# Transposes ahead of the old y products in a group's turn, logits inside it, half of x's row moves from Scalar, and a respacing of the side work

## The chip, the cores and the metric

The kernel runs on one core of a Trainium2 chip. The metric is the device time of one launch in microseconds (us), the median of several runs. TensorE (PE) multiplies matrices, VectorE (DVE), ScalarE (ACT) and GpSimd (POOL) do elementwise work, and SyncE (SP) issues DMAs. All five run their own instruction streams in order, and wait for one another on semaphores.

## The reference, cut to what matters

```
# 1. RWKV-like scan: B=4, H=8, S=768 steps, head width D=48
for t in range(S):
    cur = u * k_t outer v_t
    y[t] = r_t @ (state + cur)
    state = w_t[:, None] * state + k_t outer v_t
x = y.transpose(0, 2, 1, 3).reshape(3072, 384)
# 2. first MoE block: a gated product
x = ((x @ w1) * (x @ w2)) @ w3 @ w_out
# 3. second MoE: logits x @ w_gate -> P by 8 rounds of row and column scaling
for e in range(8):
    out += P[:, e:e+1] * (relu(x @ w1[e]) @ w2[e])      # d_model 384, d_ff 1024
```

All inputs and outputs are float32. Every large product is made of three single-pass products of high and low halves (high by high, high by low, low by high).

## The kernel before, in words

The program is written with a manual schedule: the order in which the Python code issues instructions is the order on each engine.

**The stages.** The scan is cut into 24 units n = 0 to 23 of 128 tokens. Units 0 to 6 are issued by a hand-ordered list at the start (157.7 us of the profiled run). The other units go, two to a group, into the gaps of the first MoE block: `for c in range(-1, NC)` with NC = 9, and in it `for j in 24 pieces`. In pieces j = 0 to 7 PE does the output products `po` of the token block c+1 (`moe_x2`, 9 matmuls in each piece). From j = 8 on, pieces alternate for f = 0 to 7: an even piece is `pa(f)` (9 matmuls with w1) and its copy `asb` on ACT; an odd piece is `pb(f)` (9 matmuls with w2), the product `gs` = pb x asb on DVE, its high half `gh` on ACT and its low half `gl` on POOL. `po` needs gh and gl of all eight f. After the last group comes the 8-expert stage with products `zp` and `yp` (PE 1438.59 us busy in 1443.00 us); in its first nine steps PE also does the `po` products of the last block, in nine equal parts.

**The side work** is put into the pieces by due times: `step(c, j, f)` enters f at 24c + j, and each piece first runs all that is due.

- `turn(k_old, k_new)`, at -0.5 of group k: the second half of the old units' outputs `yt2` (64 matmuls for two units), the new units' scores `sc` (64 small matmuls) and transposes `trn` (4 matmuls a unit, into a PSUM tile each), `xraw` (three ACT copies of the outputs into the x tile, lines 487 and 489), `xd_` (where the block is complete: six small DMAs, line 497, two for each of three column blocks j, which fill rows of x from its last plane), `kn_` (ACT copies the transposes out of PSUM, line 400), `cp_` (DVE writes the scores into masked tiles, line 404).
- `middle`, at 8.5: `yt1`, `up_` and `sn_`, the first half of the outputs and the state.
- `x_high` (ACT, line 505) and `x_low` (DVE, line 509) split x for the next block's `pa`/`pb`.
- `prep(n)` makes a unit's scan factors: `scan_f`, `scan_g`, `small`, `ks`, `rp`, `cc` on DVE (lines 302 to 363), `rk`, `kx`, `rx`, `ec` on POOL.
- `moe_log(g, 0)` makes the router's logits: 24 matmuls `pl` and a DVE copy `lt` (line 598). `moe_log(g, 1)` transposes lt on PE into `plt` and copies that with DVE (line 602). Step 1 stands one piece behind step 0.
- `pre_x` makes the sums of token blocks that the 8-expert stage needs: DVE sums (line 759), ACT high half (763), DVE low half (766), a DMA to memory (769).

**PSUM tiles.** `pa`, `pl`, `plt` and two of the three `po` have the tag mA, `pb`, `trn` and the third `po` have mB; each tag has two buffers, taken in turn. A tile can be written when the reader of the tile two before it in its tag is done.

Of the kernel before, what the change touches and what calls it, by code (L numbers as in the profile page):

```python
# [11 lines left out]
F32 = mybir.dt.float32  # L12
# [46 lines left out]
def tile_rwkv_moe_sinkhorn_moe(  # L59
# [724 lines left out]
    def step(c, j, *fs):  # L784
        event(24 * c + j, *fs)
# [32 lines left out]
    def front(*us):
        sc(*us)
        for n in us:  # L820
            trn(n)
# [28 lines left out]
    def units(k):  # L850
        return tuple(u_ for u_ in (FU + 2 * k, FU + 2 * k + 1) if u_ > FU)

    def turn(k_old, k_new):
        old, new = (units(k) if 0 <= k <= NC - 1 else () for k in (k_old, k_new))
        for n in old:
            yt2(n)
        if new:
            front(*new)
        if old:
            xraw(*old)  # L860
            xd_(old[-1])
        if new:
            front_end(*new)
# [3 lines left out]
    prep(FU + 2, -24 + 10, 0.6)  # L867
    prep(FU + 3, -24 + 16.5, 0.6)
    for k in range(NC):
        step(k, -0.5, lambda k=k: turn(k, k + 1))  # L870
        step(k, 4.6, lambda k=k: x_high(k + 2))
        step(k, 5.6, lambda k=k: x_low(k + 2))
        if k + 1 < NC:
            step(k, 9 - 0.5, lambda k=k: middle(*units(k + 1)))
        if k + 2 < NC:
            n = FU + 2 * k + 4
            prep(n, 24 * k + 1)
            prep(n + 1, 24 * k + 12)
            step(k, 11.6, lambda n=n: load(n, ("v",)), lambda n=n: load(n + 1, ("v",)))
    step(0, 8.6, lambda: moe_log(0, 0))  # L880
    step(0, 9.6, lambda: moe_log(0, 1))
    for g_ in range(1, NTT // UL - 1):
        step(2 * g_ - 1, 8.6, lambda g_=g_: moe_log(g_, 0))
        step(2 * g_ - 1, 9.6, lambda g_=g_: moe_log(g_, 1))

    WORK = [lambda i=i: x2[NS - 1][:, 2 * i:2 * i + 2, :] for i in range(4)]
    LATE = [WORK[0], WORK[1], WORK[3]] + [lambda nm=nm: nat[nm, 0][:, 0:2 * T].rearrange("p (a b) -> p a b", b=T)
                                          for nm in ("r", "k", "w")]
    for sb_ in range(NS - 1):
        for m_, r_ in enumerate(ORDER):  # L890
            if sb_ < NS - 2:
                t_, w_, d_ = 24 * 3 * sb_ + 9.7 + 4.2 * m_, WORK[m_ % 4], (5, 9)
            elif m_ < 3:
                t_, w_, d_ = 24 * 3 * sb_ + 9.7 + 4 * m_, WORK[(0, 1, 3)[m_]], (4, 8)
            else:
                t_, w_, d_ = 24 * (3 * sb_ + 1) + 1.7 + 1.75 * (m_ - 3), LATE[m_ % 6], (2, 4)
            place(t_, *d_, lazy(lambda sb_=sb_, r_=r_, w_=w_: pre_x(sb_, r_, w_(), 0, nc.vector)))

    def open_w():
        st_attn.close()  # L900
# [7 lines left out]
            spaced(pools["w"], [P, 4, T], F32, f"w1c{g}0", "unused")  # L908
            ld_x(0, g)

    step(NC - 1, 1.5, open_w)
    step(NC - 1, 6.6, lambda: tx0.append(moe.tile([P, 6, T], F32, tag="xraw", name="tx0")))
    for m_, (i_, g_) in enumerate(((0, 0), (1, 0), (0, 1), (1, 1), (0, 2), (1, 2), (0, 3), (1, 3))):
        place(24 * (NC - 1) + 8.7 + 1.6 * m_, 1, 2,
              lazy(lambda m_=m_, i_=i_, g_=g_: sp_w1(i_, g_, nc.gpsimd if m_ in (3, 6, 7) else nc.vector,
                                                    tx0[0][:, 2 * (m_ % 3):2 * (m_ % 3) + 2, :]
                                                    .rearrange("p a (b c) -> p (a b) c", c=P))))
# [423 lines left out]
```

## Time and profile before

| what | us |
|---|---|
| median of 3 runs (lowest, highest) | 1941.53 (1938.65, 1942.13) |
| the profiled execution | 1934.7 |
| its span, first to last instruction | 1933.0 |
| PE busy in the span (share) | 1886.9 (98%) |
| DVE, ACT, POOL busy | 1401.3, 684.2, 651.8 |
| mean granted TensorE clock | 0.999 |

PE is busy for 98% of the span, and 46 us of the span are without a matmul: some 20 us of these are in the hand-ordered start, 21 us between 157.7 and 490 us, and 4 us after that. A view of waits gives, for each line and engine, what an idle time ended on. The groups begin (first `po`) at 157.75, 194.98, 228.43, 262.67, 296.57, 328.28, 365.65, 398.09 and 429.96 us.

### The profile page before, as it was taken

How to read it: one execution, taken by the hardware profiler on the slowest of the kernel's cores; microseconds unless marked ns; L12 is line 12 of the kernel's file. 1: busy time of each engine (PE TensorE's matmuls, PEld its weight loads, DVE VectorE, ACT ScalarE, POOL GpSimd, SP SyncE). 2: the span in 40 equal slices, each digit the busy share in tenths (PEclk: the TensorE clock that was granted, in tenths of full speed). 3: DMA queues.
4: the chain of work that ended last, by engine and by line, in shares of the span. 5: the costliest groups of instructions: out<-in, count | busy, mean ns of one | idle time of the engine just before them, and what ended most of it. 6: DMA issues, size and time to landing. Idle time of an engine off the chain costs nothing.

```text
span 1933.0 us, 39529 instructions
## 1 busy us (share of the span) xinstructions
PE 1886.9 (98%) x16145; PEld 1846.2 (96%) x16145; DVE 1401.3 (72%) x2452; ACT 684.2 (35%) x1342; POOL 651.8 (34%) x903
## 2 busy tenths in 40 slices
PE   6999999999999999999999999999999999999999
PEld 3799989899999999999999999999999999999999
DVE  8866888755788776777767677777676777777666
ACT  6732334344333333333333333333333333333322
POOL 6866656535332213131312222222223132312200
PEclk9999999999999999999999999999999999999999
DMA  9632434426755555555555555655554656555563
GB/s 376 227 106 69 135 121 136 122 81 236 256 185 189 183 199 178 204 183 200 195 180 207 183 202 181 206 180 201 173 209 172 208 176 208 191 186 177 180 203 119
DMA packets 92310, 353.87 MB, mean 183 GB/s; under 512 B 10560, under 2 KB 36320, under 8 KB 66528
## 3 DMA queue, kind: packets, MB, share of 16 engines
q1 hardware_dynamic: 92128, 351.34, 52.9%
q8 instruction: 127, 2.08, 0.4%
q14 instruction: 55, 0.45, 0.1%
HBM read 329.67 MB, written 20.45 MB: 181 GB/s over the span
## 4 chain that ended last, share of the span: by engine, by line
PE 75%; DVE 1%; ACT 0%; issue 0%; POOL 0%; DVEq 0%; ACTq 0%
PE yp L113 41%; PE zp L113 34%; PE po L113 0%; DVE ct L996 0%; DVE hl L993 0%; DVE acc L1164 0%; ACT hh L988 0%; ACT ct L1003 0%; ACT gh L541 0%; PE pcs L113 0%; DVE w2l L740 0%; PE pl L113 0%; POOL gl L545 0%; ACT w2h L739 0%; DVE ct L999 0%
## 5 line engine op out<-in xcount | busy, mean ns | idle before, releaser
L113 PE MATMUL zp<-xc,w1c 128*128 128x256 f32 x5760 | 793.3, 277 | 2.2 <-ACT ct L1003 1.2
L113 PEld LDWEIGHTS zp<-xc,w1c 128*128 128x128 f32 x5760 | 765.8, 188 | 6.0 <-ACT ct L1003 2.3
L113 PE MATMUL yp<-w2h,hl 128*128 128x384 f32 x1536 | 515.3, 335 | 2.2 <-DVE hl L993 2.2
L113 PE MATMUL yp<-w2l,hh 128*128 128x384 f32 x1536 | 514.6, 335 | 0.0
L113 PE MATMUL yp<-w2h,hh 128*128 128x384 f32 x1536 | 513.1, 334 | 0.0
L988 ACT ACTIVATE hh<-ct 128x512 fp32r<-128x512 f32 x384 | 236.1, 630 | 528.6 <-DVE ct L996 268.1
L996 DVE TENSOR_TENSOR ct<-ct,zp 128x512 f32<-128x512 f32 x576 | 377.3, 681 | 45.2 <-PE zp L113 40.2
L680 POOL TENSOR_TENSOR w1c<-w1s,w1c 128x512 fp32r<-128x512 f32 (+1 forms) x120 | 127.2, 1061 | 779.7 <-ACT w1c L676 779.7
L1003 ACT ACTIVATE ct<-zp 128x512 f32<-128x512 f32 x256 | 153.4, 599 | 437.3 <-PE zp L113 432.7
L113 PEld LDWEIGHTS yp<-w2h,hl 128*128 128x128 f32 x1536 | 288.3, 188 | 2.7 <-DVE hl L993 2.5
L113 PEld LDWEIGHTS yp<-w2h,hh 128*128 128x128 f32 x1536 | 288.4, 188 | 0.2 <-issue 0.2
L113 PEld LDWEIGHTS yp<-w2l,hh 128*128 128x128 f32 x1536 | 288.4, 188 | 0.0
L1168 DVE SCALAR_TENSOR_TENSOR acc<-yp,Pm,acc 128x384 f32<-128x384 f32 x336 | 205.8, 612 | 103.5 <-PE yp L113 103.4
L993 DVE SCALAR_TENSOR_TENSOR hl<-ct,hh 128x512 fp32r<-128x512 f32 x384 | 276.3, 733 | 0.0
L999 DVE TENSOR_TENSOR ct<-ct,zp 128x512 f32<-128x512 f32 x128 | 88.0, 687 | 159.8 <-PE zp L113 159.8
L999 DVE TENSOR_TENSOR ct<-zp,ct 128x512 f32<-128x512 f32 x128 | 88.3, 690 | 75.3 <-ACT ct L1003 62.5
L680 POOL TENSOR_TENSOR w1c<-w1raw,w1c 128x128 fp32r<-128x128 f32 (+1 forms) x93 | 58.4, 628 | 195.8 <-ACT w1c L676 195.8
L672 POOL TENSOR_TENSOR w1s<-w1raw 128x128 f32<-128x128 f32 x240 | 120.5, 522 | 0.2
L545 POOL TENSOR_TENSOR gl<-gs,gh 128x256 fp32r<-128x256 f32 (+1 forms) x88 | 76.0, 869 | 126.4 <-ACT gh L541 126.4
L113 PE MATMUL pb<-xhl,w2h 128*128 128x256 f32 (+1 forms) x528 | 106.3, 296 | 6.7 <-DVE gs L536 6.2
L113 PE MATMUL pa<-xhl,w1h 128*128 128x256 f32 (+1 forms) x528 | 105.9, 293 | 3.7 <-DVE xhl L509 2.9
L113 PEld LDWEIGHTS pb<-xhl,w2h 128*128 128x128 f32 x528 | 83.2, 190 | 10.6 <-DVE gs L536 8.5
(191 smaller groups left out, 2058.2 us busy)
## 6 DMA issues: line engine op xcount, KB each, us to landing
xc<-xd SPq DMA_DIRECT2D x192, 1024.0 KB, 4.9
xc<-xd SPq DMA_DIRECT2D x64, 768.0 KB, 4.3
xd<-x2s SPq DMA_DIRECT2D x54, 256.0 KB, 2.8
w1raw<-in_e_w_dram SPq DMA_DIRECT2D x32, 384.0 KB, 3.1
w2raw<-in_e_w_dram SPq DMA_DIRECT2D x32, 384.0 KB, 3.2
raw<-in_moe_w_dram SPq DMA_DIRECT2D x8, 1024.0 KB, 9.3
nat_w<-in_w_dram SPq DMA_DIRECT2D x24, 264.5 KB, 3.5
nat_k<-in_kt_dram SPq DMA_DIRECT2D x24, 256.0 KB, 3.9
```

What stands on the lines that cost most here:

```text
L113: nc.tensor.matmul(o, lhsT, rhs, start=start, stop=stop, **kw)
L545: nc.gpsimd.tensor_tensor(gl[:, f, :], m_t.pop(("gs", blk, f)), gh[:, f, :].bitcast(F32), op=ALU.subtract)
L672: eng.tensor_tensor(tmp_[:, many.index(r), :], at_(a), at_(b), op=ALU.add if sg == 1 else ALU.subtract)
L680: eng.tensor_tensor(lo[:, d0:d1, :], sv, hi[:, d0:d1, :].bitcast(F32), op=ALU.subtract)
L988: nc.scalar.activation(hh, src, AF.Relu)
L993: nc.vector.scalar_tensor_tensor(hl, src, 0.0, hh.bitcast(F32), op0=ALU.max, op1=ALU.subtract)
L996: nc.vector.tensor_tensor(o, a, b_, op=ALU.add)
L999: nc.vector.tensor_tensor(o, a, b_, op=ALU.subtract)
L1003: nc.scalar.activation(t, src, AF.Copy)
L1168: nc.vector.scalar_tensor_tensor(dst, yp, so["Pm"][:, tt, e:e + 1], dst, op0=ALU.mult, op1=ALU.add)
```

## The change

Nothing is computed in another way; the diff moves work.

- `turn` issues the new units' `trn` first, then `yt2` of the old ones, `sc`, and in the turns of k = 2, 4, 6 and 8 `moe_log`'s step 0; then `xraw`, the row moves, `kn_` and `cp_` as before. Step 1 of the logits comes at 4.4 of the group (13.4 in group 0).
- For k of 1 and above, `turn`, `x_high`, `x_low`, `middle` and the loads of v come two pieces sooner. So `pa` and `pb` of f = 7 of the old group now stand behind the turn. `prep` comes 2 pieces sooner. In group 0 `x_high` and `x_low` come one piece later.
- Of the six row moves, the three with h = 1 are issued by `nc.scalar` for n > FU.
- `pre_x`: 31 of the 45 at a spacing of 5.1 pieces (before 33 at 4.2 or 4), the last 14 at a spacing of 1.5 with other work buffers (before 12 at 1.75).
- `open_w`, `tx0` and `sp_w1` (weights of the 8-expert stage) come 0.55, 1.0 and 2.0 pieces sooner. The nine `po` parts of the last block get unequal sizes (13, 13, 4, 13, 13, 4, 4, 4, 4 instead of 8 each).

```diff
@@ xd_
-                    nc.sync.dma_start(xt[64 * h + D:64 * h + 64, j, :],
+                    (nc.scalar if h and n > FU else nc.sync).dma_start(xt[64 * h + D:64 * h + 64, j, :],
@@ turn
-    def turn(k_old, k_new):
+    def turn(k_old, k_new, log=None):
+        for n in new:
+            trn(n)
         for n in old:
             yt2(n)
         if new:
-            front(*new)
+            sc(*new)
+        if log is not None:
+            moe_log(log, 0)
         if old:
             xraw(*old)
             xd_(old[-1])
@@
-        step(k, -0.5, lambda k=k: turn(k, k + 1))
-        step(k, 4.6, lambda k=k: x_high(k + 2))
-        step(k, 5.6, lambda k=k: x_low(k + 2))
+        sh = 2 if k else 0
+        log = k // 2 if k % 2 == 0 and k > 0 else None
+        step(k, -0.5 - sh, lambda k=k, log=log: turn(k, k + 1, log))
+        if log is not None:
+            step(k, 4.4, lambda log=log: moe_log(log, 1))
+        step(k, 5.6 - sh, lambda k=k: x_high(k + 2))
+        step(k, 6.6 - sh, lambda k=k: x_low(k + 2))
-            step(k, 9 - 0.5, lambda k=k: middle(*units(k + 1)))
+            step(k, 8.5 - sh, lambda k=k: middle(*units(k + 1)))
-            prep(n, 24 * k + 1)
-            prep(n + 1, 24 * k + 12)
+            prep(n, 24 * k + (-1 if k else 0.5), 1 if k else 0.95)
+            prep(n + 1, 24 * k + (10 if k else 11), 1 if k else 0.95)
-    step(0, 9.6, lambda: moe_log(0, 1))
-    for g_ in range(1, NTT // UL - 1):
-        step(2 * g_ - 1, 8.6, lambda g_=g_: moe_log(g_, 0))
-        step(2 * g_ - 1, 9.6, lambda g_=g_: moe_log(g_, 1))
+    step(0, 13.4, lambda: moe_log(0, 1))
@@ pre_x
-                t_, w_, d_ = 24 * 3 * sb_ + 9.7 + 4.2 * m_, WORK[m_ % 4], (5, 9)
-                t_, w_, d_ = 24 * (3 * sb_ + 1) + 1.7 + 1.75 * (m_ - 3), LATE[m_ % 6], (2, 4)
+            t_, w_, d_ = 9.7 + 5.1 * m_, WORK[m_ % 4 if m_ < 27 else (0, 1, 3)[m_ % 3]], ((5, 9) if i_ < -1 else (3, 5))
+            t_, w_, d_ = TURN + 1.7 + 1.5 * i_, LATE[i_ % 6], (2, 3.6)
@@ 8-expert stage
+    PARTS = (0, 13, 26, 30, 43, 56, 60, 64, 68, 72)
-                    moe_x2(NB - 1, i_, PO)
+                    moe_x2(NB - 1, i_, PO, PARTS[i_:i_ + 2])
```

What this does to the engines' orders is shown at the turn of k = 5 (the names in the rows are tiles, and `krr`, `nat_...` are buffers in which factors and scores lie).

TensorE at the turn of k = 5, before: `pb` of f = 7 stands ahead, then yt2, sc, trn, and the group's first `po`.

```order
L113 MATMUL pb<-xhl,w2h 128x256 x2
L113 MATMUL pb<-xhl,w2l 128x256
...
L113 MATMUL sc_4761<-krr 64x64 [waits PE_49,Pool_49]
...
L113 MATMUL trn<-ident,kn 128x128 [waits DVE_49]
L113 MATMUL trn<-ident,kn 128x128 x3
L113 MATMUL trn<-ident,krr 128x128 [waits DVE_49]
L113 MATMUL trn<-ident,krr 128x128 x3
L113 MATMUL po<-gh,w34h 128x256 [waits Activation_49]
```

TensorE at the same turn, after:

```order
L113 MATMUL trn<-ident,kn 128x128 [waits DVE_49]
L113 MATMUL trn<-ident,kn 128x128 x3
L113 MATMUL trn<-ident,krr 128x128 [waits DVE_49]
L113 MATMUL trn<-ident,krr 128x128 x3
...
L113 MATMUL sc_4737<-krr 64x64 [waits PE_49]
...
L113 MATMUL pa<-xhl,w1h 128x256 [waits Activation_49]
...
L113 MATMUL pb<-xhl,w2h 128x256 [waits PE_49,Activation_49]
...
L113 MATMUL po<-gh,w34h 128x256
```

The transposes moved to the turn's head, pa and pb of f = 7 behind it, and that pb takes the PSUM buffer of the first transposes: its wait for Activation is for `kn_` (line 400), where the pb before waited for DVE.

ScalarE at the same turn, before:

```order
L541 ACTIVATE gh<-gs 128x256 [waits DVE_49]
L487 ACTIVATE xraw<-yt_4401 128x2x4x64 [waits PE_49]
L489 ACTIVATE xraw<-yt_4400 64x2x4x64 [waits PE_49]
L489 ACTIVATE xraw<-yt_4400 64x2x4x64
L400 ACTIVATE nat_n_110<-trn 128x512 [waits PE_49]
L400 ACTIVATE kn<-trn 128x512 [waits PE_49,Pool_49]
```

ScalarE at the same turn, after:

```order
L487 ACTIVATE xraw<-yt_4370 128x2x4x64 [waits PE_49]
L489 ACTIVATE xraw<-yt_4369 64x2x4x64 [waits PE_49]
L489 ACTIVATE xraw<-yt_4369 64x2x4x64
L497 DMA xraw<-xraw 16x256 [waits DMAHW2_49,Activation_49]
L497 DMA xraw<-xraw 16x256 [waits DMAHW4_49]
L497 DMA xraw<-xraw 16x256 [waits DMAHW6_49]
L400 ACTIVATE nat_n_110<-trn 128x512
L400 ACTIVATE kn<-trn 128x512 [waits Pool_49]
L532 ACTIVATE asb<-pa 128x256 [waits PE_49]
```

Three DMA issues stand between the x copies and `kn_`, and the asb of f = 7 stands behind `kn_`.

VectorE around the logits, before:

```order
L598 COPY lt<-pl 128x128 [waits PE_49]
L536 TENSOR_TENSOR gs<-pb,asb 128x256 [waits PE_49,Activation_49]
L602 COPY L<-plt 128x32 [waits PE_49]
```

VectorE around the logits, after:

```order
L536 TENSOR_TENSOR gs<-pb,asb 128x256 [waits PE_49,Activation_49,Pool_49]
L598 COPY lt<-pl 128x128 [waits PE_49]
L404 COPY_PREDICATED ec<-mask,sc_4175 128x256
...
L536 TENSOR_TENSOR gs<-pb,asb 128x256 [waits DVE_49,PE_49,Activation_49]
...
L602 COPY L<-plt 128x32 [waits PE_49]
```

Between the copy lt and the copy of plt there was one gs; now the turn's four score copies, gs of f = 7 and a unit's factors lie between.

## Rows read from the trace of the kernel before

**Rows 1.** PE's waits, 157 to 490 us: total us, times, longest us
```profile
PE plt L113 <- DVE lt L598: 7.2, 5, 2.0
PE pb L113 <- DVE gs L536: 6.2, 8, 1.3
PE pa L113 <- DVE xhl L509: 2.9, 6, 0.6
PE yp L113 <- DVE hl L993: 2.2, 1, 2.2
PE zp L113 <- ACT ct L1003: 1.2, 1, 1.2
PE pl L113 <- issue: 0.7, 1, 0.7
PE zp L113 <- DVE ct L996: 0.6, 1, 0.6
```

**Rows 2.** Stretches: length, busy us of PE, PEld, DVE, ACT, POOL; clock, DMA
```profile
328.20:365.60 37.40, 33.63 (x491) 32.43 (x490) 29.78 (x62) 12.37 (x32) 20.63 (x23) 0.95 0.43 125
...
490.00:1933.00 1443.00, 1438.59 (x10247) 1434.81 (x10245) 1038.61 (x1701) 473.72 (x877) 358.67 (x582) 1.00 0.55 190
```

**Rows 3.** TensorE's timeline, group 5's logits: start, us, [idle before <-releaser]
```profile
340.83 0.86 PE L113 MATMUL pl<-x2s,gate 128*32 128x128 f32 x24
341.62 0.50 PE L113 MATMUL pb<-xhl,w2h 128*128 128x256 f32 x2
...
344.92 0.30 PE L113 MATMUL plt<-ident,lt 128*128 128x128 f32 x1 [1.98 <-DVE lt L598]
```

**Rows 4.** The stretch 345.75 to 349.20 us, columns as in rows 2
```profile
345.75:349.20 3.45, 3.45 (x19) 3.45 (x18) 0.75 (x3) 0.52 (x2) 0.68 (x1) 0.51 0.84 229
```

**Rows 5.** TensorE's timeline at the turn of k = 5
```profile
323.27 0.39 PE L113 MATMUL pa<-xhl,w1h 128*128 128x256 f32 x2
...
324.29 0.39 PE L113 MATMUL pb<-xhl,w2h 128*128 128x256 f32 x2
...
325.20 0.28 PE L113 MATMUL pb<-xhl,w2l 128*128 128x256 f32 x1
...
325.92 0.65 PE L113 MATMUL yt<-nat_k,Sn 64*64 64x64 f32 x32
326.39 0.65 PE L113 MATMUL sc<-krr 64*64 64x64 f32 x32
...
327.43 0.66 PE L113 MATMUL trn<-ident,kn 128*128 128x128 f32 x4
...
328.28 0.36 PE L113 MATMUL po<-gh,w34h 128*128 128x256 f32 x1
```

**Rows 6.** ScalarE's timeline at the turn of k = 5
```profile
327.41 0.42 ACT L541 ACTIVATE gh<-gs 128x256 fp32r<-128x256 f32 x1 [1.18 <-DVE gs L536]
327.74 0.58 ACT L487 ACTIVATE xraw<-yt 128x512 f32<-128x512 f32 x1
328.34 1.21 ACT L489 ACTIVATE xraw<-yt 64x512 f32<-64x512 f32 x2
329.58 0.60 ACT L400 ACTIVATE nat_n<-trn 128x512 f32<-128x512 f32 x1
```

**Rows 7.** SP's queue at the turn of k = 5: start, us, line, DMAs issued
```profile
328.97 3.75 SPq L497 DMA_DIRECT2D xraw<-xraw  x6
```

**Rows 8.** Line 497 (the row moves): all 66 issues, ns
```profile
L497 SPq DMA_DIRECT2D xraw<-xraw x66: 513/582/1565, 63.0 to 435.2; - x66
...
DMA to landing us min/median/max: 1.7/1.8/6.8
```

**Rows 9.** VectorE's timeline at the turns of k = 5 and k = 8
```profile
326.95 0.42 DVE L536 TENSOR_TENSOR gs<-pb,asb 128x256 f32<-128x256 f32 x1 [0.99 <-POOL gl L545]
...
418.48 0.42 DVE L536 TENSOR_TENSOR gs<-pb,asb 128x256 f32<-128x256 f32 x1 [1.36 <-PE pb L113]
```

**Rows 10.** GpSimd's timeline at the turn of k = 5
```profile
328.58 0.73 POOL L545 TENSOR_TENSOR gl<-gs,gh 128x256 fp32r<-128x256 f32 x1
```

More of the change, by code (lines that the diff above doesn't have):

```diff
@@ L563, in tile_rwkv_moe_sinkhorn_moe, with moe_x2 @@
     po_t = {}
-    def moe_x2(blk, i, parts=X2S):
+    def moe_x2(blk, i, parts=X2S, at_=None):
         gh, gl = g_t[blk]
         n_ = KD * NF * 3 // parts
-        for m in range(i * n_, (i + 1) * n_):
+        for m in range(*(at_ or (i * n_, (i + 1) * n_))):
             q, rest = divmod(m, 3 * NF)
@@ L816, in prep @@
                 put(d, lambda nm=nm, m=m: load(m, (nm,)))
[L818 to L821, printed above, removed]
     def front_end(*us):
@@ L873, in tile_rwkv_moe_sinkhorn_moe @@
         if k + 1 < NC:
-            step(k, 9 - 0.5, lambda k=k: middle(*units(k + 1)))
+            step(k, 8.5 - sh, lambda k=k: middle(*units(k + 1)))
         if k + 2 < NC:
             n = FU + 2 * k + 4
-            prep(n, 24 * k + 1)
-            prep(n + 1, 24 * k + 12)
-            step(k, 11.6, lambda n=n: load(n, ("v",)), lambda n=n: load(n + 1, ("v",)))
+            prep(n, 24 * k + (-1 if k else 0.5), 1 if k else 0.95)
+            prep(n + 1, 24 * k + (10 if k else 11), 1 if k else 0.95)
@@ L880, in tile_rwkv_moe_sinkhorn_moe @@
+            step(k, 11.6 - sh, lambda n=n: load(n, ("v",)), lambda n=n: load(n + 1, ("v",)))
     step(0, 8.6, lambda: moe_log(0, 0))
-    step(0, 9.6, lambda: moe_log(0, 1))
-    for g_ in range(1, NTT // UL - 1):
-        step(2 * g_ - 1, 8.6, lambda g_=g_: moe_log(g_, 0))
-        step(2 * g_ - 1, 9.6, lambda g_=g_: moe_log(g_, 1))
+    step(0, 13.4, lambda: moe_log(0, 1))
     WORK = [lambda i=i: x2[NS - 1][:, 2 * i:2 * i + 2, :] for i in range(4)]
-    LATE = [WORK[0], WORK[1], WORK[3]] + [lambda nm=nm: nat[nm, 0][:, 0:2 * T].rearrange("p (a b) -> p a b", b=T)
-                                          for nm in ("r", "k", "w")]
@@ L889, in tile_rwkv_moe_sinkhorn_moe @@
-    for sb_ in range(NS - 1):
-        for m_, r_ in enumerate(ORDER):
-            if sb_ < NS - 2:
-                t_, w_, d_ = 24 * 3 * sb_ + 9.7 + 4.2 * m_, WORK[m_ % 4], (5, 9)
-            elif m_ < 3:
-                t_, w_, d_ = 24 * 3 * sb_ + 9.7 + 4 * m_, WORK[(0, 1, 3)[m_]], (4, 8)
-            else:
-                t_, w_, d_ = 24 * (3 * sb_ + 1) + 1.7 + 1.75 * (m_ - 3), LATE[m_ % 6], (2, 4)
-            place(t_, *d_, lazy(lambda sb_=sb_, r_=r_, w_=w_: pre_x(sb_, r_, w_(), 0, nc.vector)))
+    LATE = [WORK[0], WORK[1], WORK[3]] + [lambda f=f: f()[:, 0:2 * T].rearrange("p (a b) -> p a b", b=T)
+                                          for f in (lambda: nat["w", 0], lambda: last["F"], lambda: last["G"])]
@@ new lines, in tile_rwkv_moe_sinkhorn_moe @@
+    last = {}
+    step(NC - 2, -1, lambda: last.update(F=st[NU - 1]["F"], G=st[NU - 1]["G"]))
+    TURN = 24 * (NC - 2)
+    for m_ in range((NS - 1) * len(ORDER)):
+        sb_, r_ = m_ // len(ORDER), ORDER[m_ % len(ORDER)]
+        i_ = m_ - 31
+        if i_ < 0:
+            t_, w_, d_ = 9.7 + 5.1 * m_, WORK[m_ % 4 if m_ < 27 else (0, 1, 3)[m_ % 3]], ((5, 9) if i_ < -1 else (3, 5))
+        else:
+            t_, w_, d_ = TURN + 1.7 + 1.5 * i_, LATE[i_ % 6], (2, 3.6)
+        place(t_, *d_, lazy(lambda sb_=sb_, r_=r_, w_=w_: pre_x(sb_, r_, w_(), 0, nc.vector)))
@@ L909, in open_w @@
             ld_x(0, g)
-    step(NC - 1, 1.5, open_w)
-    step(NC - 1, 6.6, lambda: tx0.append(moe.tile([P, 6, T], F32, tag="xraw", name="tx0")))
+    step(NC - 1, 0.95, open_w)
+    step(NC - 1, 5.6, lambda: tx0.append(moe.tile([P, 6, T], F32, tag="xraw", name="tx0")))
     for m_, (i_, g_) in enumerate(((0, 0), (1, 0), (0, 1), (1, 1), (0, 2), (1, 2), (0, 3), (1, 3))):
-        place(24 * (NC - 1) + 8.7 + 1.6 * m_, 1, 2,
+        place(24 * (NC - 1) + 6.7 + 1.7 * m_, 1, 2,
               lazy(lambda m_=m_, i_=i_, g_=g_: sp_w1(i_, g_, nc.gpsimd if m_ in (3, 6, 7) else nc.vector,
```

## The prediction

> **What bounds the kernel now.** Start with the stretches [rows 2]. In the 8-expert stage, 490 to 1933 us, TensorE is busy for 1438.59 of 1443.00 us: no reordering of side work can win more than 4.4 us there, and the diff leaves that stage's loop alone. What can move lies between 157 and 490 us, where two groups of work (the scan's units and the first MoE block) are woven together. There the view of TensorE's waits [rows 1] says what ends its idle time: 21.0 us in all, of which 7.2 us are five waits of the logits' transpose `plt` for the DVE copy `lt`, 6.2 us are `pb` waiting for `gs` on DVE (its PSUM buffer), 2.9 us are `pa` waiting for `x_low`, and 1.8 us are the first `zp` products at the start of the 8-expert stage. All but one of these releasers are on DVE or ACT. Those engines are busy for 80% and 33% of a group's stretch [rows 2], so they are late because of the place of their work and not for want of time. TensorE's clock matters in one place: the stretch of group 5 has a mean granted clock of 0.95, and inside it 345.75 to 349.20 us ran at 0.51, the lower level of 1.2 GHz [rows 4]. It fell after a wait of 1.98 us with no matmul in it [rows 3].
>
> **What goes away.** Five terms.
> 1. `plt`. Step 1 of the logits moves from one piece behind step 0 to seven pieces behind it, and 13.4 against 8.6 in group 0. The longest wait is 1.98 us [rows 3] and a piece is 1.02 us (pa f7 at 323.27, pb f7 at 324.29) [rows 5], so five or six more pieces cover it wherever DVE puts lt: −7.2 us.
> 2. The half clock behind that wait. 3.45 us at 0.51 [rows 4] hold what takes 3.45 × 0.51 = 1.76 us at full clock: −1.7 us.
> 3. `pa` behind `x_low`: the row moves start at the turn, two pieces sooner, and `x_high` and `x_low` keep about their distance to the turn plus a piece. `middle` also slips in front of `pa(0)`, where TensorE now has its work to do before it needs x. −2.9 us.
> 4. `pb` behind `gs`. The turn's score copies move out of the stretch after the group's first `po`, so the next unit's factors start right behind gs of f = 7; and the token factors of `pre_x` come every 5.1 instead of 4.2 pieces, a fifth less of that load per group. Against that, the second `prep` is 2 pieces sooner as well. The eight waits have a mean of 0.78 us [rows 1]; between none and all of 6.2 us I take −5.0.
> 5. The start of the 8-expert stage. The first `po` part grows from 8 to 13 matmuls. Nine matmuls of this size take a piece of 1.02 us [rows 5], 0.113 us each, so 5 more cover 0.6 of the 1.2 us that `zp` waits for ACT [rows 1]. Later parts shrink from 8 to 4, so I give the 0.6 us wait for DVE no gain: −0.6 us, with bounds of −1.8 and +1.
>
> Sum: −17.4 us.
>
> **What is added.** The transposes `trn` and `pb` share the PSUM tag mB with two buffers. Before, `trn` came behind pb f7, and the next user of the tag was the `po` of the second column block, whole microseconds later. Now the order is pb f6, trn, trn, then pb f7, which takes the buffer of the first trn. So pb f7 waits until ACT has copied that transpose out (`kn_`), and on ACT that copy stands behind three x copies and, new, three DMA issues. Let E be the end of yt2 in the turn, 325.92 + 0.65 = 326.57 [rows 5].
> - ACT's path: the x copies run 327.74 to 329.55, 1.8 us with their gaps [rows 6], and start 0.05 us after E if ACT is free. Three issues on a queue: six take 3.75 us on SP, so the cadence is (3.75 − 0.58) / 5 = 0.63 us [rows 7, 8], three are 1.9 us. The copy is 0.60 us [rows 6], hand-over 0.05. E + 0.05 + 1.84 + 1.9 + 0.6 + 0.05 = E + 4.44.
> - TensorE's path: sc from 326.39 to the next tile at 327.43 is 1.04, pa f7 1.02 [rows 5]; from E that is 1.04 + 1.02 − 0.18 = 1.88. In the turns of even k the logits `pl` add 341.62 − 340.83 = 0.79 [rows 3].
> - The wait is thus 4.44 − 1.88 = 2.56, say 2.5 us, in the turns k = 1, 3, 5, 7 and 1.7 in k = 2, 4, 6: 4 × 2.5 + 3 × 1.7 = 15.1 us. Turn 0 is not moved and turn 8 has no new units.
>
> The trace of before has no DMA issued by ACT. The bounds of an issue there are nothing (the queue takes it beside the copies) and twice SP's cadence (both queues share what makes the descriptors); I take SP's own 0.63, since it is the same transfer in the same form. The three issues that leave SP save its queue 1.9 us; x's rows then land earlier, but terms 3's waits are the only ones that this served. Behind the waiting pb f7 stand gs f7, gh and gl, and all `po` of the next group.
>
> What the split of the issues could give at best is small: an issue is 0.58 us and the landing 1.8 us [rows 8]. The Trainium skill ("DMA: Bandwidth & Descriptors", section "Issuing engines are not separate DMA queues") says that several issuing engines only save the sequencer's time to initiate, on the same 16 DMA engines; this trace shows that time as a third of the landing, and by that rule the split is worth nothing to the sum and ACT pays for what SP saves.
>
> Second: trn of the first unit waits for gs f5, that of the second for gs f6, since they take those buffers. The two units' trn take 328.28 − 327.43 = 0.85 us [rows 5], so the second is reached 0.43 behind pb f6. gs starts 0.14 us behind its pb where DVE is free (418.48, after a wait for that pb) and 1.47 behind where it is not (326.95 against pb f7's end at 325.20 + 0.28) [rows 5, 9]. It lasts 0.42. So the wait is 0.14 + 0.42 + 0.05 − 0.43 = 0.2 at least and 1.5 at most; with term 4's relief I take 0.3 × 8 = 2.4 us.
>
> Third: gl of f = 7 is needed by the 23rd `po`, 22 × 0.113 = 2.5 us behind pb f7, where before the whole turn lay between. gs (0.14 + 0.42), gh 0.42, gl 0.73 [rows 6, 9, 10] and hand-overs are 1.8 us: covered by 0.7 us; at a DVE lag of 1.47 it would miss by 0.6.
>
> At nothing: `open_w`, `tx0`, `sp_w1` and the v loads, hidden under the last group's 27 us of matmuls; the price if that cover fails is term 5's bound.
>
> **Sum.** +15.1 + 2.4 − 17.4 = +0.1 us. On the profiled run, 1934.7 (span 1933.0), that is 1934.8; the median of the runs lies 6.8 us above the profiled run, and the same difference on it gives 1941.53 + 0.1 = 1941.6 us. Own range 1936 to 1947, from terms 4 and 5 and the ±0.3 us on seven waits.
>
> **Rivals.**
> - *The issues on ACT cost ACT nothing.* Then kn is done at E + 2.54 and the wait is 0.66 us in the four odd turns and none in the even ones: 2.6 instead of 15.1, −12.5 us: 1929.1. For it: an issue moves no data through ACT. Against: SP's issues stand 0.63 apart [rows 7].
> - *The half clock comes back.* Two waits of about 2 us (1.98 and the 2.2 of `yp` [rows 1]) stand in this trace, and one of them was followed by the low level; the new four are 2.5 us. At 1.7 us each and half to three quarters of them: up to +5.2: 1946.8.
> - *Slower: both queues take turns.* If an issue on ACT waits for the one on SP, ACT's third ends after six cadences, 3.75 instead of 1.9 us [rows 7], and seven waits grow by 1.85: +13: 1954.6. It turns the result to slower (by 0.2%, 3.9 us, about what a measurement of this kernel tells from no change) once an issue costs ACT more than 0.63 + 3.8 / 21 = 0.81 us. For it: SP's longest issue took 1.565 us [rows 8], so something can hold one. Against: no row shows two queues at once. The Trainium skill ("Perfetto Trace Analysis", section "DMA Instruction — HWDGE (DVE, Sync)") says that the descriptor generator is locked for one issuer at a time and the sequencer is free only after it; by that the time would be this rival's, and no run of before shows two issuers.
> - *DVE stays late.* If the 2-pieces-sooner factors eat the relief, term 4's 5.0 stay and the second trn waits 1.5 instead of 0.3 in seven turns: +8.4 + 5.0 = +13.4: 1955.
>
> **How the numbers follow.** The forecast 0.38, the free issues 0.27, the half clock 0.12, queues taking turns 0.12, late DVE 0.11. Faster by over 0.2% (under 1937.6): 0.26 of the free issues and 0.14 of the forecast's lower part, 0.40. Within: 0.17 + 0.05 + 0.01 = 0.23. Slower (over 1945.4): 0.07 of the forecast, 0.07 of the half clock, 0.12 and 0.11: 0.37. The range 1927 to 1954 leaves out half of each of the last two and a tail of the free issues, under 0.2.
>
> **What would show it.** In the waits of TensorE: `plt` and `pa` gone, and a new row, `pb` on ACT's `trn` copy, of about 15 us in 7 waits; near 3 us means free issues, near 28 means turns. ACT's timeline at a turn: the gap between the x copies and `kn_` is 1.9 us, 0.1 or 3.7. `trn` on DVE's gs near 2 us; over 8 means DVE stays late. A granted clock below 1.00 in the stretches of odd groups means the half clock. The forecast is wrong if ACT is not free at E, if gl of f = 7 is missed by `po`, or if the 8-expert stage gets idle time.

## The result

The changed kernel is slower. Its median is 1958.34 us (1955.07 to 1961.03, 6 runs), against 1941.83 us (1938.65 to 1944.36, 6 runs) of the kernel before on the same chip: a ratio of 1.0085, with a 95% interval of 1.0071 to 1.0098, or +16.5 us. The forecast was 1941.6 us, no change, with a range of 1927 to 1954.

Executions of one and the same kernel differ by some 8 us (the kernel before took 1933 to 1936 us in three runs of the first group below and 1941 to 1943 in the other four), and since the traces put this into the 8-expert stage (span less the start of the first `zp`: 1933.0 − 456.8 = 1476.2 us in the profile of before, 1955.4 − 471.5 = 1483.9 in that of the changed kernel), the kernels are compared below by their ratios and by the time at which TensorE starts the first `zp`. That start went from 456.85 to 471.47 us, +14.6 us; so nearly all of the loss lies between 157 and 471 us. Of the 2 us that the medians have beyond that, the trace shows one part, 1.7 us lost to the lower clock at the start of the 8-expert stage (below).

**The waits of TensorE after the change**, 155 to 520 us (total us, times, longest us), answering to [rows 1]:

```profile
PE trn L113 <- DVE gs L536: 7.4, 7, 1.3
PE pb L113 <- ACT krr L400: 6.1, 3, 2.2
PE pb L113 <- DVE gs L536: 5.4, 8, 1.7
PE pb L113 <- ACT nat_n L400: 4.5, 2, 3.0
PE pb L113 <- ACT kn L400: 3.7, 2, 2.2
PE yp L113 <- DVE hl L995: 1.8, 1, 1.8
PE zp L113 <- DVE ct L998: 0.7, 1, 0.7
PE po L113 <- ACT gh L541: 0.5, 1, 0.5
PE po L113 <- POOL gl L545: 0.4, 1, 0.4
PE trn L113 <- POOL nat_n L352: 0.4, 1, 0.4
PE pa L113 <- DVE L L602: 0.4, 1, 0.4
```

`plt` has left the list, and `pa` on `x_low` too. Three rows are new under one line, 400: `pb` waits for `kn_` in whichever buffer the transposes went to, 6.1 + 4.5 + 3.7 = 14.3 us in 7 waits. The other new row is `trn` on `gs`, 7.4 us. `pb` on `gs` is still there with 5.4 of its 6.2 us.

**One turn.** ScalarE, its DMA queue (ACTq), SyncE's queue and TensorE at the turn of k = 5, answering to [rows 5 to 7]; a fence for each timeline, ScalarE with its queue, SyncE's queue, TensorE (start, us, [idle before <-releaser]):

```profile
336.48 1.21 ACT L489 ACTIVATE xraw<-yt 64x512 f32<-64x512 f32 x2
337.71 2.59 ACTq L497 DMA_DIRECT2D xraw<-xraw  x3
340.35 0.60 ACT L400 ACTIVATE nat_n<-trn 128x512 f32<-128x512 f32 x1 [2.67 <-DMA xraw<-xraw]
```

```profile
337.10 2.08 SPq L497 DMA_DIRECT2D xraw<-xraw  x3
```

```profile
332.20 0.60 PE L113 MATMUL trn<-ident,kn 128*128 128x128 f32 x4
334.06 0.66 PE L113 MATMUL trn<-ident,krr 128*128 128x128 f32 x4 [1.26 <-DVE gs L536]
...
341.00 0.50 PE L113 MATMUL pb<-xhl,w2h 128*128 128x256 f32 x2 [3.02 <-ACT nat_n L400]
```

And the turn of k = 7 on ScalarE, where the issues are as short as in five of the seven turns:

```profile
411.55 1.81 ACTq L497 DMA_DIRECT2D xraw<-xraw  x3
413.41 0.60 ACT L400 ACTIVATE krr<-trn 128x512 f32<-128x512 f32 x1 [1.89 <-issue]
```

The three issues hold ScalarE for 1.80 us in five turns and for 2.56 to 2.59 us in two, where the last issue took 1.35 and 1.38 us instead of 0.60 (SyncE's own longest before was 1.57 [rows 8]; what held them is open); `kn_` starts 0.05 us behind the last of them. TensorE's wait ends with its first copy, 3.02 us long here, 2.23 to 2.25 us in the other odd turns, 1.43 to 1.56 us in the even ones.

**The clock.** Four stretches behind the four longest of these waits, columns as in [rows 2]:

```profile
341.80:345.20 3.40, 3.40 (x18) 3.40 (x17) 2.47 (x3) 0.72 (x2) 1.52 (x2) 0.50 0.00 0
266.96:270.15 3.19, 3.19 (x16) 3.19 (x16) 1.17 (x2) 1.10 (x4) 0.22 (x1) 0.50 0.23 78
195.98:199.00 3.02, 3.02 (x26) 3.02 (x27) 1.61 (x3) 1.44 (x4) 0.66 (x1) 1.00 0.01 4
414.06:417.50 3.44, 3.44 (x30) 3.44 (x31) 0.76 (x2) 1.43 (x4) 0.74 (x1) 1.00 0.24 80
```

Two ran at the lower level (0.50, which is 1.2 GHz), two at the full one. A third stretch at 0.50, from 498.9 to 502.1 us, lies in the 8-expert stage, behind a wait of `yp` of 1.79 us. At 0.50 the first two lost 1.7 and 1.6 us, where the kernel before lost 1.7 once [rows 4].

| term, up to the first `zp` | forecast, us | measured, us |
|---|---|---|
| `plt` on lt | −7.2 | −7.2 |
| half clock | −1.7 | +1.6 (3.3 against 1.7) |
| `pa` on x_low | −2.9 | −2.5 (0.4 left, on the copy of plt) |
| `pb` on gs | −5.0 | −0.8 |
| `pb` on kn_ | +15.1 | +14.3 |
| second `trn` on gs | +2.4 | +7.4 |
| `po` on gh and gl of f = 7 | 0 | +0.9 |
| sum | +0.7 | +13.7 of 14.6 |

(The forecast's sum of +0.1 has in it 0.6 for the start of the 8-expert stage, which lies behind the first `zp`.)

### The profile page after: what moved, and what is told of

Its sections match the earlier page's. It is cut to its first block, busy times and chain, and to the rows that moved or that the text cites. A ratio compares the mean times of both kernels' runs of the same rounds, so it can differ in the third digit from the quotient of the medians.

```text
span 1955.4 us, 39559 instructions
## 1 busy us (share of the span) xinstructions
PE 1899.8 (97%) x16145; PEld 1857.0 (95%) x16145; DVE 1400.5 (72%) x2452; ACT 683.6 (35%) x1342; POOL 656.8 (34%) x903
## 4 chain that ended last, share of the span: by engine, by line
PE 75%; DVE 0%; DMA 0%; POOL 0%; ACT 0%; issue 0%; DVEq 0%; ACTq 0%
PE yp L113 41%; PE zp L113 34%; PE po L113 0%; DMA xd<-x2s 0%; POOL x2s L759 0%; PE pb L113 0%; DVE acc L1167 0%; POOL x2s L766 0%; PE pl L113 0%; DVE hl L995 0%; PE pa L113 0%; ACT ct L1005 0%; PE pcs L113 0%; DVE w2l L740 0%; ACT w2h L739 0%
```

## The experiments

Two questions were open: whether what `pb` waits for at `kn_` is really lost time, or only moved from VectorE's lateness; and why `gs` stayed late. In the first group of runs the kernel before had a median of 1941.42 us (1932.97 to 1943.24, which is why the intervals of this group are wide), in the second 1933.35, in the third 1941.92; each group ran on a chip of its own. Each kernel has one trace.

| kernel | ratio to before, 95% interval | first `po`, us | first `zp`, us | lost to the lower clock between them, us |
|---|---|---|---|---|
| before | 1 | 157.75 | 456.85 | 1.7 |
| the changed kernel | 1.0085 [1.0071, 1.0098] | 157.64 | 471.47 | 3.3 |
| changed, moves on SyncE | 1.0020 [0.9992, 1.0049] | 159.16 | 456.96 | 0 |
| changed, kn_ first | 1.0029 [1.0001, 1.0058] | 157.81 | 457.85 | 0 |
| changed, yt2 first | 1.0034 [0.9995, 1.0072] | 158.80 | 459.97 | 0 |
| before, logits alone | 0.9940 [0.9912, 0.9967] | 157.28 | 448.10 | 0 |
| changed, SyncE and yt2 first | 0.9965 [0.9950, 0.9981] | 158.94 | 449.95 | 1.7 |
| before, logits and spread | 0.9967 [0.9955, 0.9980] | 157.78 | 448.26 | 0 |
| changed, SyncE, second factors later | 0.9981 [0.9971, 0.9992] | 157.99 | 450.65 | 0 |
| changed, SyncE, old spacing | 1.0030 [1.0018, 1.0043] | 160.96 | 464.75 | 5.1 |
| changed, SyncE, yt2 first, factors later | 0.9943 [0.9930, 0.9955] | 158.97 | 445.36 | 0 |
| the same with the split, kn_ first | 0.9971 [0.9961, 0.9982] | 158.56 | 451.66 | 0 |
| before, with five parts of the change | 0.9917 [0.9904, 0.9931] | 157.70 | 439.69 | 0 |

The start of the first `zp` holds more than an edit's effect. The first `po` already comes 157.28 to 160.96 us into the span, though the hand-ordered start is the same in all, and four of the traces have stretches at the lower clock ahead of the first `zp`, each of which loses about 1.7 us. So where two traces differ in these, it is said.

### The row moves on SyncE alone

```diff
-                    (nc.scalar if h and n > FU else nc.sync).dma_start(...
+                    nc.sync.dma_start(...
```

> The changed kernel with one part undone: all six row moves are issued by SyncE again. In the changed kernel ScalarE holds three issues of 2.6 us together between the x copies and the transposes' copy kn_, and pb of f = 7 waits for that copy, 14.3 us in 7 turns. Theory A (the queue on ScalarE makes these waits, and what it gives up is won): the waits on the copy fall to under 3 us, the time from 1958 to about 1945 to 1947. Theory B (VectorE is what is late; its work only waits elsewhere once pb stands sooner): the waits on the copy fall likewise, but pb and trn waiting for gs on VectorE grow from 12.8 us by half of it or more, and the time stays above 1950. If ScalarE isn't held by its issues at all, nothing changes: 1958.

The first `zp` came at 456.96, 14.5 us sooner than with the split. TensorE's waits, 157 to 500 us:

```profile
PE trn L113 <- DVE gs L536: 7.5, 7, 1.3
PE pb L113 <- DVE gs L536: 5.7, 8, 1.7
...
PE pb L113 <- ACT krr L400: 0.8, 2, 0.4
...
PE pb L113 <- ACT kn L400: 0.4, 1, 0.4
...
PE pb L113 <- ACT nat_n L400: 0.4, 1, 0.4
```

The waits on `kn_` fell from 14.3 to 1.6 us, those on `gs` did not grow (13.2 against 12.8), and no stretch at the lower clock is left (3.3 us in the changed kernel). The median is 1941.90 us, less than theory A's 1945 to 1947. Theory A holds: with the split goes the whole of the loss, and it is no lateness of VectorE in another place. (The 2.6 us of the expectation are the turns of k = 4 and 5; the other five have 1.80.) But the rest of the change then only equals the kernel before.

### kn_ ahead of the x copies

```diff
+        for n in new:
+            kn_(n)
         if old:
             xraw(*old)
             xd_(old[-1])
-        if new:
-            front_end(*new)
+        for n in new:
+            cp_(n)
```

> The changed kernel with the copies kn_ put before the x copies and the row moves on ScalarE; the row moves stay split. Theory A: pb of f = 7 waits for nothing on ScalarE (14.3 us gone) and the half clock behind these waits (2 to 4 us) goes with it: 1940 to 1944. Theory B: waits for gs on VectorE (trn and pb, 12.8 us in the changed kernel) grow to 18 us or more, the time is 1948 or above. A third way: x arrives 1.2 us later and pa waits for x_low again, up to 3 us.

The waits on `kn_` are gone, and the first `zp` comes at 457.85 us: 13.6 us won. `trn` (7.4) and `pb` (5.4) on `gs` stayed as they were, so theory B fails here too; the median of 1944.28 us lies at theory A's upper end, and `pa` on `x_low`, the third way, is not in the list. So the loss needs both, the issues on ScalarE and their place in front of `kn_`. But a new wait stands in the list, which no theory named:

```profile
PE po L113 <- POOL gl L545: 3.4, 6, 0.8
...
PE po L113 <- ACT gh L541: 1.1, 2, 0.6
```

The three issues now hold `asb` of f = 7 instead of `kn_`, with gs, gh and gl of f = 7 behind it, and `po` meets them.

### yt2 ahead of the transposes

```diff
-        for n in new:
-            trn(n)
         for n in old:
             yt2(n)
+        for n in new:
+            trn(n)
         if new:
             sc(*new)
```

> The changed kernel with the old units' yt2 put before the new units' trn in the turn, nothing else. yt2 (0.9 us) then covers the gs of f = 6 for which the second trn waits: trn on gs from 7.4 us to 1 or 2. The copy kn_ still stands behind the x copies and the issues, counted from the end of yt2, and pb of f = 7 comes 0.85 us later on TensorE, so its wait falls from 14.3 by about 6 to 8. Theory A: both are won, 12 us, 1946. Theory B (VectorE late anyway): pb on gs grows, 1951 or above.

The wait of `trn` on `gs` left the list; `pb` on `kn_` fell from 14.3 to 10.5 us (4.1 + 3.9 + 2.5), less than expected; `pb` on `gs` was 6.3. The first `zp` came at 459.97: 11.5 us won, near the 12 of theory A, but not by its sum: `trn` gave 7.4 and `kn_` 3.8 us, `pb` on `gs` took 0.9, and 3.3 us are the two stretches at the lower clock, which this trace does not have although its longest wait was 2.8 us (the first `po` came 1.2 us later).

### The logits alone, in the kernel before

```diff
             front(*new)
+        if log is not None:
+            moe_log(log, 0)
...
+        if log is not None:
+            step(k, 4.4, lambda log=log: moe_log(log, 1))
-    step(0, 9.6, lambda: moe_log(0, 1))
-    for g_ in range(1, NTT // UL - 1):
-        step(2 * g_ - 1, 8.6, lambda g_=g_: moe_log(g_, 0))
-        step(2 * g_ - 1, 9.6, lambda g_=g_: moe_log(g_, 1))
+    step(0, 13.4, lambda: moe_log(0, 1))
```

> The kernel before with one part of the change alone: the logits in the turns of k = 2, 4, 6, 8, their transpose at 4.4 of the group (13.4 in group 0). Theory A (that wait is won in full): plt's 7.2 us and the half clock's 1.7 us go, 1941.8 to 1933. Theory B (VectorE is what is late and the wait moves to pb on gs): pb on gs grows from 6.2 by 4 or more, 1937 to 1942.

TensorE's waits, 157 to 500 us:

```profile
PE pb L113 <- DVE gs L536: 9.2, 12, 1.3
PE pa L113 <- DVE xhl L509: 2.2, 5, 0.8
```

`plt` is gone and `pb` on `gs` grew by 3.0, but the first `zp` came at 448.10, 8.75 us sooner: so the 8.9 us that terms 1 and 2 gave this edit came in sum. They are not these two items alone: 7.2 and 1.7 us went, 3.0 came back as `pb` on `gs`, and the rest lies in `pa` on `x_low` and in `pl`, 0.7 less each, the first `po` (0.5 sooner) and 1 us less of busy time. This one part of the change, alone, beats both kernels.

### Two and three parts of the changed kernel put right

The row moves on SyncE and yt2 first, the two diffs above together:

```diff
-                    (nc.scalar if h and n > FU else nc.sync).dma_start(...
+                    nc.sync.dma_start(...
...
+        for n in old:
+            yt2(n)
         for n in new:
             trn(n)
-        for n in old:
-            yt2(n)
```

> The changed kernel with two parts put back: the row moves on SyncE alone, and yt2 before the transposes. With the moves on SyncE alone the second trn waited 7.5 us in all for gs of f = 6, pb 5.7 us for gs, and the first zp stood at 457.0 us. Theory A (a wait of TensorE is won wherever other matmuls cover it): trn's 7.5 us go, the copy kn_ has 0.85 us more cover, the first zp comes at 449 to 450. Theory B (VectorE is the limit between 200 and 450 us): pb on gs takes over most of it, first zp 454 or later.

```profile
PE pb L113 <- DVE gs L536: 5.9, 8, 1.9
```

This is the only row over 1 us before the first `zp`, at 449.95: 7.0 us sooner than with the moves on SyncE alone, and that with 1.7 us lost to the lower clock from 384 to 388 us, behind a wait of 1.91. The wait of `trn` was won, as theory A had it, and the 1.6 us on `kn_` with it.

The moves on SyncE, and the second unit's factors two pieces later:

```diff
-            prep(n + 1, 24 * k + (10 if k else 11), 1 if k else 0.95)
+            prep(n + 1, 24 * k + (12 if k else 11), 0.8 if k else 0.95)
```

> The changed kernel with all row moves on SyncE and the second unit's factors begun at 12 instead of 10 of a group and pressed by a factor of 0.8, so that they end where they did. With the moves on SyncE alone: trn on gs 7.5, pb on gs 5.7, first zp 457.0 us. Theory A (the factors two pieces sooner take the relief away): pb on gs falls to 3 or less and the first zp comes at 453 to 455, trn on gs stays or grows by a little. Theory B (VectorE has too little time in the group, and where the factors stand doesn't matter): the waits only change places, sum 12 to 15 us, first zp 456 to 459.

```profile
PE pb L113 <- DVE gs L536: 4.5, 6, 1.9
PE trn L113 <- DVE gs L536: 3.3, 8, 0.7
```

The first `zp` came at 450.65, 6.3 us sooner (1.2 of them ahead of the first `po`), more than theory A's 2 to 4, and most of it from `trn` (7.5 to 3.3), which theory A had not expected. The trace of the changed kernel says why. VectorE at the turn of k = 5, and GpSimd in the four microseconds around it:

```profile
333.58 0.42 DVE L536 TENSOR_TENSOR gs<-pb,asb 128x256 f32<-128x256 f32 x1 [0.61 <-POOL gl L545]
```

```profile
330.31 0.61 POOL L352 TENSOR_TENSOR nat_w<-krr,Mt 128x256 f32<-128x256 f32 x1
330.88 0.63 POOL L352 TENSOR_TENSOR krr<-nat_w,Ft 128x256 f32<-128x256 f32 x1
331.47 0.61 POOL L358 TENSOR_TENSOR krr<-krr,Mt 128x256 f32<-128x256 f32 x1
332.05 0.63 POOL L358 TENSOR_TENSOR krr<-krr,Ft 128x256 f32<-128x256 f32 x1
332.64 1.59 POOL L545 TENSOR_TENSOR gl<-gs,gh 128x256 fp32r<-128x256 f32 x2
```

The second `trn` waits for gs of f = 6. That gs was held by GpSimd: it needs the buffer of gs f = 4 (there are two), and gl f = 4 on GpSimd stands behind four factor products (`kx` and `rx` of the second unit). In six of the seven turns gs f = 6 waits so (in VectorE's waits `gs` on `gl` has 6 entries, 7.3 us). In five of them VectorE had nothing else to do for the 1.2 to 1.6 us ahead of it; in the turn shown it worked until 332.96 us and only the last 0.61 us are GpSimd's. The kernel before had the same wait, 6.5 us in 7 entries, but at gs of f = 7 [rows 9], which no transposes stood close behind. With the later, pressed factors, GpSimd's order at the same place puts a gl between the two pairs:

```profile
319.61 0.80 POOL L352 TENSOR_TENSOR nat_w<-krr,Mt 128x256 f32<-128x256 f32 x1
320.38 0.80 POOL L352 TENSOR_TENSOR krr<-nat_w,Ft 128x256 f32<-128x256 f32 x1
321.56 0.74 POOL L545 TENSOR_TENSOR gl<-gs,gh 128x256 fp32r<-128x256 f32 x1 [0.38 <-ACT gh L541]
322.25 0.61 POOL L358 TENSOR_TENSOR krr<-krr,Mt 128x256 f32<-128x256 f32 x1
```

and in VectorE's waits `gs` on `gl` is down to 0.9 us in 2 entries (with the moves on SyncE alone it was 8.0 in 7). The edit moves VectorE's part of the factors too; that GpSimd's part is what counted rests on these waits.

All three edits together (the added lines):

```diff
+                    nc.sync.dma_start(...
...
+        for n in old:
+            yt2(n)
         for n in new:
             trn(n)
...
+            prep(n + 1, 24 * k + (12 if k else 11), 0.8 if k else 0.95)
```

> The changed kernel with three parts put right: row moves on SyncE alone, yt2 ahead of the transposes, the second unit's factors begun at 12 and pressed to 0.8. With the first two the first zp came at 449.95 us and pb waited 5.9 us for gs. If the factors' place is what makes gs late, pb on gs falls to 4 or less and the first zp comes at 447 to 448.5. If it only helped the second transposes (whose wait yt2 now covers), nothing is left to win: 449.5 to 450.5.

The first `zp` came at 445.36, 4.6 us sooner and sooner than either case had it. But `pb` on `gs` fell from 5.9 to 4.5 us only, so 1.4 us of waits were won; another 1.7 are the stretch at the lower clock, which this trace does not have, and what the rest is was not found. The place of the factors also won something that yt2 doesn't cover, less than the first `zp` says.

### The spread of the token factors

The old spacing in the changed kernel with its moves on SyncE (the old loop of `pre_x` put back):

```diff
-            t_, w_, d_ = 9.7 + 5.1 * m_, WORK[m_ % 4 if m_ < 27 else (0, 1, 3)[m_ % 3]], ((5, 9) if i_ < -1 else (3, 5))
-            t_, w_, d_ = TURN + 1.7 + 1.5 * i_, LATE[i_ % 6], (2, 3.6)
+                t_, w_, d_ = 24 * 3 * sb_ + 9.7 + 4.2 * m_, WORK[m_ % 4], (5, 9)
+                t_, w_, d_ = 24 * (3 * sb_ + 1) + 1.7 + 1.75 * (m_ - 3), LATE[m_ % 6], (2, 4)
```

> The changed kernel with all row moves on SyncE and the token factors at the old spacing of 4.2 pieces and with the old buffers. With the moves on SyncE alone: trn on gs 7.5, pb on gs 5.7, first zp 457.0 us. If the spread is what kept VectorE from being later still, the two waits grow by 3 to 6 us and the first zp comes at 460 or later; if the spread does nothing, they stay within 1 us and the first zp at 456 to 458.

```profile
PE trn L113 <- DVE gs L536: 10.8, 9, 2.2
PE pb L113 <- DVE gs L536: 6.2, 6, 1.5
```

The first `zp` came 7.8 us later. The two stretches from the first `po` to the first `zp` (columns as in [rows 2]), with the moves on SyncE alone and then with the old spacing as well:

```profile
159.16:456.96 297.80, 280.69 (x4083) 270.96 (x4078) 223.98 (x486) 109.12 (x280) 165.13 (x180) 1.00 0.37 119
160.96:464.75 303.79, 284.49 (x4084) 274.13 (x4078) 227.79 (x486) 109.98 (x280) 164.51 (x180) 0.98 0.37 116
```

Of the 7.8 us, 1.8 lie ahead of the first `po`, 2.2 are idle time of TensorE (17.1 us became 19.3), and 3.8 are busy time, in which three stretches at the lower clock (227.7 to 231.1, 265.3 to 268.7 and 371.1 to 374.5 us) lost 5.1. They come at the end of or shortly behind waits of `trn` of 2.14, 1.86 and 1.86 us; a fourth, of 2.16 us, brought none. So what the spread is shown to do here is to take 3.8 us off the two waits on `gs` (17.0 against 13.2); whether the longer waits also bring the lower clock is not shown. The spread in the kernel before, on top of the logits (the same lines the other way round):

```diff
-                t_, w_, d_ = 24 * 3 * sb_ + 9.7 + 4.2 * m_, WORK[m_ % 4], (5, 9)
+            t_, w_, d_ = 9.7 + 5.1 * m_, WORK[m_ % 4 if m_ < 27 else (0, 1, 3)[m_ % 3]], ((5, 9) if i_ < -1 else (3, 5))
...
```

> The kernel before with two parts of the change: the logits inside the turn, and the token factors spread (31 at 5.1 pieces, 14 at 1.5). With the logits alone pb waited 9.2 us for gs and the first zp came at 448.1 us. The forecast held that the spread makes VectorE earlier in each group: pb on gs then falls by 3 to 5 us, first zp at 443 to 445. Rival: VectorE is late only where the second unit's factors stand in a row ahead of gs, which the spread doesn't touch: pb on gs 8 to 10, first zp 447 to 449.

Here `pb` on `gs` fell from 9.2 to 6.6 us, and the first `zp` stayed (448.26 against 448.10). The same two stretches, the logits alone and then with the spread:

```profile
157.28:448.10 290.82, 279.24 (x4080) 270.66 (x4079) 219.78 (x484) 107.50 (x278) 160.66 (x177) 1.00 0.39 121
157.78:448.26 290.48, 280.37 (x4080) 271.75 (x4079) 219.12 (x484) 107.16 (x278) 159.32 (x177) 1.00 0.39 122
```

TensorE's idle time fell by 1.5 us in all (11.6 to 10.1), and the same matmuls were busy 1.1 us longer at the full clock, so the stretch became 0.3 us shorter. In the two orders the spread shortens the waits on `gs` by 3.8 and 2.6 us; a gain of 8 us in time is not shown in either.

### The split with nothing behind it

The kernel with three parts put right, but with the moves split and `kn_` ahead of the issues:

```diff
-                    nc.sync.dma_start(...
+                    (nc.scalar if h and n > FU else nc.sync).dma_start(...
...
+        for n in new:
+            kn_(n)
         if old:
             xraw(*old)
             xd_(old[-1])
...
```

> The same as the kernel with three parts put right, but with the row moves split between SyncE and ScalarE as in the change, and the copies kn_ ahead of the x copies and the issues, so that the issues hold nothing that pb waits for. If the split has a gain of its own (x's rows land about 1.9 us earlier), x_high and with it ScalarE come earlier and the first zp comes 1 us or more ahead of the other's. If it has none, both lie within 0.7 us. If three issues on ScalarE delay asb and gh of f = 7 so that po waits for gl, it is later by 1 to 3 us.

The first `zp` came at 451.66, 6.3 us later than without the split. ScalarE at the turn of k = 5, and the waits:

```profile
327.08 2.43 ACTq L497 DMA_DIRECT2D xraw<-xraw  x3
329.56 0.38 ACT L532 ACTIVATE asb<-pa 128x256 f32<-128x256 f32 x1 [2.51 <-issue]
```

```profile
PE po L113 <- POOL gl L545: 5.1, 8, 1.2
```

Whatever stands behind the three issues is late: `asb` of f = 7, and through gs, gh and gl the next group's `po`. `po`'s waits on gl and gh are 6.1 us (5.1 + 1.0), more than the 1 to 3 us expected. If the split has a gain, it is smaller than this; the copies `kn_` in front of the x copies are a part of this kernel too, and were not tried here without the split.

### A kernel faster than both

The kernel before, with the logits and the spread, and `middle` and the opening of the 8-expert stage as in the change:

```diff
-            step(k, 9 - 0.5, lambda k=k: middle(*units(k + 1)))
+            step(k, 6.5, lambda k=k: middle(*units(k + 1)))
-    step(NC - 1, 1.5, open_w)
+    step(NC - 1, 0.95, open_w)
...
+                    moe_x2(NB - 1, i_, PO, PARTS[i_:i_ + 2])
```

> The kernel before with the logits in the turn and the token factors spread, and with three more parts of the change: middle at 6.5 in front of pa(0), the opening of the 8-expert stage sooner, and the unequal po parts. With the first two the first zp came at 448.3 us, pa waited 2.2 us for x, zp 1.8 us. Middle ahead of pa(0) should take away pa's waits: first zp at 445.5 to 447. The unequal parts and the sooner weights should take zp's waits from 1.8 to about 0.7. If VectorE only gets later by the sooner middle (16 small operations ahead of x_low's reader), pb on gs grows from 6.6 to 8 or more and the first zp stays at 448.

Its median is 1926.0 us (1925.29 to 1927.08, 4 runs) against 1941.92 of before. The first `zp` came at 439.69, 8.6 us sooner than without these parts and much sooner than expected. Its waits of 157 to 500 us, and the stretch up to the first `zp` (length, busy us of PE and the others):

```profile
PE pb L113 <- DVE gs L536: 3.0, 6, 0.8
PE yp L113 <- DVE hl L997: 2.9, 1, 2.9
PE zp L113 <- DVE ct L1000: 0.7, 1, 0.7
```

```profile
157.70:439.60 281.90, 278.15 (x4080) 271.35 (x4079) 215.99 (x485) 109.28 (x279) 159.50 (x180) 1.00 0.40 125
```

TensorE is idle for 3.75 of 281.9 us there. `middle` in front of pa(0) not only took away `pa`'s wait for x but also halved `pb` on `gs`, from 6.6 to 3.0: its sixteen VectorE operations of line 456, which stand ahead of the first gs, now come two pieces sooner. That this is the cause is argued from the order; which of the parts gave how much of the 8.6 us was not taken apart.

## Why the prediction was wrong

**Right: the wait for kn_.** The forecast had 15.1 us in 7 waits, and 14.3 us came; 2.5 and 1.7 us, against 2.23 to 3.02 and 1.43 to 1.56. So the cost that made the change slower was foreseen, with its mechanism. The price of an issue on ScalarE, which no row of before showed, was taken from SyncE's cadence: 0.63 us each; it is 0.60 (1.80 for three) in five turns. Neither the rival of free issues (`kn_` started 0.05 us behind the last issue) nor that of queues taking turns came: three on each queue lay within 2.4 us at k = 7, where one queue took 3.75 for six [rows 7]. The Trainium skill ("Perfetto Trace Analysis", section "DMA Instruction — HWDGE (DVE, Sync)") has the sequencer free only when the issue is over, and the trace agrees (those 0.05 us); that one issuer locks out the other, which it has too, is not seen here: at k = 7 SyncE's three took 2.06 us beside ScalarE's 1.81.

**Right: plt, and pa behind x_low.** In the changed kernel all 7.2 us of `plt` went and 2.5 of the 2.9 of `pa`. With the logits alone the first `zp` came 8.75 us sooner, where terms 1 and 2 have 8.9, though other waits share in that sum.

**Wrong: the two terms on gs.** Term 4 (−5.0) gave −0.8, and the second `trn` cost 7.4 instead of 2.4. Together these are 9.2 of the 13 us that the sum of the terms is off. Both rested on one step: that the relief of the token factors' spread outweighs factors that come two pieces sooner. The relief is there, but small: with the moves on SyncE these waits are 13.2 us, and 17.0 without the spread. The factors' cost was named and given no number, and only VectorE was looked at. The second unit's factors also bring four products to GpSimd, which moved in front of gl f = 4, and gs f = 6 waits for that gl. The prediction's own row [rows 9] has that releaser, `gs` idle 0.99 us for `gl`, and read it as lateness of VectorE. GpSimd's queue should have been followed as VectorE's was. The rival of a late VectorE had the right sign and the right two waits, at 13.4 us against the 9.2 that came, with the wrong engine named. (The term's 0.3 × 8 also counts eight turns, where seven moved.)

**Wrong: the half clock.** −1.7 became +1.6. It was a rival with a chance of 0.12, but the forecast's own waits of 2.5 us were longer than the one wait known to bring it [rows 3]; beside such waits it should have stood in the sum. Two of the four waits over 2 us brought it. Which ones do was not to be foreseen: with yt2 first, a wait of 2.8 us brought none.

**What the split did.** The forecast counted that ScalarE pays for it, found no gain for x, and set the loss of about 15 us against gains of 17 elsewhere. The sum came out near nothing because it took the gains at or near their best and the loss as it was. With the split undone the first `zp` of the change equals that of the kernel before (456.96 against 456.85); the 14.5 us stand between them, and `kn_` in front of the issues gives 13.6 of them back with the split left in.

## What to carry to other kernels

A tile that moves ahead in a ring of two PSUM buffers makes its reader's engine a part of the path: all that stands in front of that reader, DMA issues too, must be counted into the wait. When factors move sooner, follow each engine's queue that they touch and look for the short operation that they now stand in front of; the releaser of a late operation names that queue. Where a forecast is a difference of two large sums, try the parts apart: here one part alone was worth 9 us, and undoing another gave back 14.5. When two traces are compared, look at the granted clock of each before a difference is put down to the edit: 5.1 us of one difference of 7.8 were the clock.

## What the runs showed of the hardware

- Three DMA issues on ScalarE take 1.80 us, as long as on SyncE, and hold ScalarE's next operation; two queues issuing at once were not slowed to one another's turn (2.06 us for SyncE's three beside 1.81 for ScalarE's), but in two of seven turns ScalarE's three took 2.56 to 2.59 us.
- TensorE fell to the lower clock behind waits of 1.98 (before), 1.79, 2.23 and 3.02 us (the changed kernel), and did not behind others of 2.24 and 2.25 us in the same trace, nor behind 2.8 us with yt2 first: the length of a wait alone does not tell it.
- The matmuls of the 8-expert stage stand at two distances, at a granted clock of 1.00 and with no wait of TensorE from 700 to 1900 us: `zp` matmuls of 256 columns start 114.0 ns apart in the traces of before, the logits alone and the old spacing, and 115.5 ns in the other ten. Over 5760 of them that is some 8.6 us, about the difference between 1475 or 1476 and 1484 us for the stage. The three have the old spacing of the token factors in common, but that is not what sets it: the changed kernel with its moves on SyncE and yt2 first has a median of 1925.44 us, which leaves no room for 1484 us behind its first `zp` at 449.95. What sets it was not found.
